# Retention in split halves from chunk 6 on instead of chunk 8, in a retention and two-layer feed-forward kernel

## The chip, the cores and the metric

The kernel runs on one core of one Trainium2 chip. The metric is the device time of one execution in microseconds (us); the figure to compare is the median of several executions. Profiles name the engines PE (TensorE matmul), PEld (TensorE weight load), DVE (VectorE), ACT (ScalarE), POOL (GpSimd) and SP (SyncE, which issues most DMAs).

## What is computed

Three stages, in fp32, follow one another:

```
state = gamma * state + k[t] (outer) v[t]          # retention, 4 batches, 8 heads, 768 steps, head size 64
y[t]  = scale * q[t] @ state
x = y as [3072, 512]
h = x @ w_in;  x = elu(h) @ w_out                  # first layer, 512 -> 2048 -> 512
h = x @ w2_in; x = (P(h) / Q(h)) @ w2_out          # second layer, P cubic, Q quadratic in |h|
```

Retention is worked in 24 chunks of 128 steps, six to a batch. Inside a chunk it is a masked product of queries and keys times the values, plus the queries times the state from the chunks before; the state is then decayed and the chunk's own key-value product added.

## The kernel before

The work is done in tiles of 512 tokens (`j`, 0 to 5; four chunks each) by 128 hidden units (`f`, 0 to 15). A step `it` of the first layer takes one pair (j, f) from a written list `seq`: (0, 0..5), then (1, 0..15), then (0, 6..15), then the other tiles. In a step TensorE does `g1` (12 products into `h`), then the second half of retention (`at_out`), then `g2` of the step before (12 products into four banks `acc`), then the first half of retention for the next half chunk (`at_in`). The order on every engine is the order in which the code issues; nothing is scheduled, and each engine takes its instructions in that order.

A half chunk, `i = 2 * chunk + g`, holds four heads. Halves 0 to 9 are done ahead of the first layer. Half 10 goes with step 0, 11 with step 1, 12 and 13 (chunk 6) with steps 2 and 3, 14 and 15 (chunk 7) with steps 4 and 5. Steps 6 to 21 carry no retention; from half 16 on it goes on later. Chunk 6 is the first of its batch, so it has no state to read; chunk 7 has one.

There are two forms. The early form (`c < LATE`, `c < EARLY`) multiplies in plain fp32, adds the decayed state on TensorE by a product with a diagonal matrix (L266), and ScalarE copies the sum back into `St` (L338). VectorE only masks the scores (L299). The late form splits each operand into a high and a low part in the fp32r type and takes three products of them (`gemm3`, L392). VectorE then multiplies the scores by the mask in place (L286), ScalarE rounds them to `Ah` (L289), VectorE subtracts to get `al` (L290) and makes the low parts of the queries of the next half (`qp`, L209, two instructions). It also updates `St` (L340 copies in a batch's first chunk, L342 after it) and joins the two parts of the output (L354, or L356 where there is no state). ScalarE and GpSimd split the keys (`kf`) and values (`vf`); SP loads `kr` and `kvs` for each half, one buffer each.

Beside this, weights arrive as float64 and VectorE narrows each 128x512 block in four instructions (L113, L114, L115, L117), ScalarE rounds it (L126) and GpSimd subtracts (L127). The list `nops` says how many of the four-instruction steps VectorE does in each step: 4, 5, 5, 6, 6, 6 in steps 0 to 5, and 5 in each of steps 6 to 17. Steps 6 to 11 use again the weights of f = 0 to 5. Each step's activation also needs VectorE once (L701, `t`), behind part of the narrowing, and ScalarE and GpSimd split its result to `gh` and `gl` for `g2`. Since the list leaves tile 0 after f = 5, its four banks `acc` are copied out in step 6, two by VectorE (L457); the next `g2` writes the same banks.

Of the kernel before, what the change touches and what calls it, by code (L numbers as in the profile page):

```python
# [9 lines left out]
F32 = mybir.dt.float32  # L10
F32R = mybir.dt.float32r
# [8 lines left out]
D = 64  # L20
C = 128
NP = H // 2
NW = 12
KD = 4
KF = 16
EARLY = 8
LATE = 8
LN2_63 = 63 * float(np.log(2.0))
TINY = 2.0 ** -63
QC = float(np.float32(1.0) + np.float32(1e-6))  # L30
# [19 lines left out]
def retention_ffn_kernel(ctx: ExitStack, tc: tile.TileContext, qkT, kv, w1i, w1o, w2i, w2o, a_, b_, tab, out):  # L50
    nc = tc.nc
# [16 lines left out]
    atw = at.enter_context(tc.tile_pool(name="atw", bufs=2))  # L68
# [84 lines left out]
    chk = {}  # L153

    def load_q(c):
        if c in (2, 3, 6, 7):
            qT = half[c % 4][:, 512:1024]
        else:
            qT = atw.tile([128, 512], F32, tag="qT", name="qT")
        chk[c] = (qT.rearrange("p (a t) -> p a t", a=NP),) + (kvb[c % 4] if c < LATE else (None,) * 3)  # L160
        nc.sync.dma_start(out=chk[c][0], in_=qkT[c, :, 0])

    def load_k(c):
        qT, vw, kw, kn = chk[c]
        if c >= LATE:
            return
        if c > 1:
            nc.sync.dma_start(out=kn, in_=kv[c, :, 0])
        for e in range(2):
            r = slice(64 * e, 64 * e + 64)  # L170
            (nc.scalar if 0 < c < 4 else nc.sync).dma_start(out=kw[r, e], in_=qkT[c, r, 1])
        if c < 2:
            nc.sync.dma_start(out=kn, in_=kv[c, :, 0])
        vf = vw.rearrange("p a f d -> p (a f d)")
        mid = kv[c, :, 1, 1:7, :].rearrange("p (a e) d -> p a (e d)", e=2)
        nc.sync.dma_start(out=vf[:, 128:704].rearrange("p (a n) -> p a n", a=3)[:, :, 0:128], in_=mid)
        nc.sync.dma_start(out=vf.rearrange("p (b d) -> p b d", d=D)[:, 0:12:11, :],
                          in_=kv[c, :, 1, 0:8:7, :])
# [5 lines left out]
    def scale_k(c):  # L184
        kn = chk[c][3]
        if c % CB != CB - 1 and c < LATE:
            nc.gpsimd.tensor_tensor(out=kn, in0=kn, in1=gk_t.to_broadcast([128, H, D]), op=ALU.mult)

    def load_kr(i):
        c, g = divmod(i, 2)  # L190
        if i < NI:
            nc.sync.dma_start(out=kr, in_=qkT[c, :, 1, 2 * g:2 * g + 2])

    def prep(i):

        c, g = divmod(i, 2)
        if c < LATE or i >= NI:
            return none
# [14 lines left out]
    def load_kv(i):  # L213
        c, g = divmod(i, 2)
        if LATE <= c < NCH:
            nc.sync.dma_start(out=knv, in_=kv[c, :, :, 4 * g:4 * g + 4])

    def scale_kn(i):
        c, g = divmod(i, 2)
        if LATE <= c < NCH and c % CB != CB - 1:  # L220
            nc.gpsimd.tensor_tensor(out=knv[:, 0], in0=knv[:, 0],
# [12 lines left out]
    def x_tile(j):  # L234
        if j not in x_t:
            n = XB[j] if j in XB else (j[1] + 1) % 2
            x_t[j] = tuple(xp.tile([128, KD, 512], F32R, tag=f"{nm}{n}", name=nm) for nm in ("xh", "xl"))
        return x_t[j]

    def at_in(i, early=False):  # L240
# [15 lines left out]
        def kv_sum():  # L256
            if c % CB != CB - 1:
                for p in (0, 1):
# [4 lines left out]
                    v2 = vw[:, 2 * g + p, 0:3:2, :]  # L263
                    old = c < EARLY and c % CB != 0
                    if old:
# [60 lines left out]
    def at_state(i):  # L326
# [3 lines left out]
        def part(e, p):  # L330
            r = slice(64 * e, 64 * e + 64)
            q = 2 * g + p
            d = slice(64 * e, 64 * e + 64)
            if c % CB == 0 or c < EARLY:
                if p == 0 and c % CB != CB - 1:
                    src, dst = so[r, 2:4, d], St[r, 2 * g:2 * g + 2, d]
                    if c < EARLY:
                        nc.scalar.copy(dst, src)  # L338
# [8 lines left out]
    def at_x(i):  # L347
        c, g = divmod(i, 2)
        sc, o = ps_t.pop(i)
        if c >= LATE:  # L350
            for e in range(2):
                r = slice(64 * e, 64 * e + 64)
                if c % CB:
                    nc.vector.tensor_tensor(out=o[r, 0:2, :], in0=su[r], in1=sc[r, e:4:2, :], op=ALU.add)  # L354
                else:
                    nc.vector.tensor_copy(o[r, 0:2, :], sc[r, e:4:2, :])  # L356
        xs = [x[:, 2 * g:2 * g + 2, c % 4 * C:c % 4 * C + C] for x in x_tile(c // 4)]
        nc.scalar.copy(xs[0], o[:, 0:2, :])
        nc.vector.tensor_tensor(out=xs[1], in0=o[:, 0:2, :], in1=xs[0].bitcast(F32), op=ALU.subtract)

    def run(steps):
        for x in steps:
            x()
# [30 lines left out]
    def g1(ps, f, xh, xl):  # L394
        wh, wl = W[f, "i"]
        pairs = []
        for kc in range(KD):
            s = slice(128 * kc, 128 * kc + 128)
            pairs += [(wh[:, s], xh[:, kc, :]), (wh[:, s], xl[:, kc, :]), (wl[:, s], xh[:, kc, :])]
        gemm3(ps, pairs, True, True)  # L400
# [99 lines left out]
    k0 = atw.tile([128, 1024], F32, tag="k0", name="k0", bufs=1)  # L500
    v0, v1 = (atw.tile([128, 768], F32, tag=nm, name=nm, bufs=1) for nm in ("v0", "v1"))
    n0 = atw.tile([128, 512], F32, tag="n0", name="n0", bufs=1)
# [54 lines left out]
    def abs_next():  # L557
        narrow_a(*todo[nabs[0]])
        nabs[0] += 1
# [19 lines left out]
    for i in range(10):  # L579
        c, g = divmod(i, 2)  # L580
# [25 lines left out]
        if i in (2, 3, 4, 5, 7, 8):  # L606
            ops, end = conv_next()
            ends.append(end)
    load_q(6)
    load_k(6)  # L610
    at_out(9)
    run(at_state(9))
    at_x(9)
    done()
    abs_next()
    nc.scalar.activation(out=b1, in_=ab[:, 5:6], func=ACTF.Abs)
# [3 lines left out]
    def load_c(f, e):  # L620
        c = tmp("wc")
        nc.sync.dma_start(out=c, in_=w2s[f][e])
        W[1, f, e, "c"] = c

    qp = atw.tile([128, 2, NP, C], F32R, tag="k0", name="qp", bufs=1)
    late_kv = atw.tile([128, 768], F32, tag="v0", name="kvs", bufs=1)
    knv = late_kv[:, 0:512].rearrange("p (b h d) -> p b h d", b=2, h=4)
    su = late_kv[:, 512:768].rearrange("p (a t) -> p a t", a=2)
    al = atw.tile([128, 4 * C], F32R, tag="n0", name="al", bufs=1)
    vf = None  # L630
    def first_late():

        load_q(LATE)
        load_kr(2 * LATE)
        load_kv(2 * LATE)
        for e in range(2):
            nc.gpsimd.memset(qp[64 - 64 * e:128 - 64 * e, e].bitcast(F32), 0.0)

    half0 = 6
    seq = [(0, f) for f in range(half0)] + [(1, f) for f in range(KF)] + [(0, f) for f in range(half0, KF)]  # L640
# [37 lines left out]
    for it, (j, f) in enumerate(seq):  # L678
        last = j == NB - 1
        xh, xl = x_t[j]  # L680
        both = j == 0 and (f < half0 or f >= KF - 8)
        at_a = both or (1 < j < NB - 1 and f % 2 == 0)
        at_b = both or (1 < j < NB - 1 and f % 2 == 1)
        h = psh.tile([128, 512], F32, tag="h", name="h")
        g1(h, f, xh, xl)
        n = nops[it]
        st = []
        if at_a:
            at_mask(nx[0])
            prep(nx[0] + 1)()  # L690
        narrow(min(n, 3))
        if at_a:
            st = attn_a()
        t = tmp("t", "t")
        nc.scalar.activation(out=t, in_=h, func=ACTF.Relu, scale=-1.0)  # L695
        nc.scalar.activation(out=t, in_=t, func=ACTF.Exp, scale=-1.0)  # L696
        finish()
        run(st)
        if at_a:
            at_x(nx[0])  # L700
        nc.vector.scalar_tensor_tensor(out=t, in0=t, scalar=-1.0, in1=h, op0=ALU.add, op1=ALU.max)  # L701
        gh = gp.tile([128, 512], F32R, tag="gh", name="gh")
        gl = gp.tile([128, 512], F32R, tag="gl", name="gl")
        nc.scalar.copy(gh, t)  # L704
        nc.gpsimd.tensor_tensor(out=gl, in0=t, in1=gh.bitcast(F32), op=ALU.subtract)  # L705
        if at_a:
            split_v(nx[0] + 1)
        narrow(max(n - 3, 0))
        abs_ahead((nops + [0])[it + 1])
        fill((3 if it < half0 + 8 else 1) - (1 if stream else 0))  # L710
        if last:
            split_w(1, f, 0)
            if f + 1 < KF:
                load_c(f + 1, 0)
            if f in (3, 6, 9, 12):
                load_x2(0, f // 3 - 1)
            if f in (4, 7, 10, 13):
                split_x2(0, f // 3 - 1)
        if pend is not None:
            g2(0, *pend)  # L720
        if at_b:
            attn_b()
        if last:
            if f:
                split_w(1, f - 1, 1)
            load_c(f, 1)
        if it < half0 + 8:
            fill(2 if stream else 3)
        elif not last and it not in tuple(range(19, 32)) + (47, 63, 79):
            fill(2)  # L730
        if it == 1:
            load_q(7)
            load_k(7)
        if it == 2:
            first_late()
        if it == 3:
            vf = atw.tile([128, 2, 4, D], F32R, tag="v1", name="vf", bufs=1)
        if (j, f) == (0, KF - 1):
            load_ya()
        if j == NB - 2 and f == KF - 1:  # L740
            load_c(0, 0)
        pend = (j, f, gh, gl)
# [40 lines left out]
    for j in range(NB):  # L783
        xh, xl = x_tile((1, j))
        for f in range(KF):
            h = ph.tile([128, 512], F32, tag="h2", name="h2")
            g1(h, f, xh, xl)
            a = rational_a1(h)
# [60 lines left out]
```

## Time and profile before

| | |
|---|---|
| median of 3 executions | 1185.8 us (1184.75 to 1186.55) |
| span of the profiled execution | 1184.0 us |
| TensorE busy | 1173.0 us, 99% of the span |
| VectorE busy | 896.9 us, 76% |
| ScalarE busy | 723.0 us, 61% |
| GpSimd busy | 487.5 us, 41% |

The span runs from the first to the last instruction of the profiled execution; the timed figures stand 1.8 us above it in the median. Shares of busy time are averages over the whole program; VectorE's is far higher in the first 165 us, where the weights of the first layer are narrowed.

### The profile page before, as it was taken

Reading aid. Unit: us, or ns where it says so; the run is one execution under the profiler, and the core shown is the slowest. Engines: PE = TensorE matmul, PEld = TensorE weight load, DVE = VectorE, ACT = ScalarE, POOL = GpSimd, SP = SyncE. Lnnn points to the kernel's source line nnn. Section 1 sums busy time; section 2 is a strip of 40 time slices with the busy share of each in tenths; the row PEclk is TensorE's granted clock in tenths of the full one; section 3 lists DMA queues with packets and bytes.
Section 4 is the critical chain, followed back from the end, with each engine's and each line's share of the span. In section 5 each row is a group of like instructions: output and inputs, shape, how many; then the busy total and the mean of one; then the engine's idle time right before and its main releaser. Section 6 shows DMA issues by size and latency. Waiting matters only on the chain.

```text
span 1184.0 us, 15783 instructions
## 1 busy us (share of the span) xinstructions
PE 1173.0 (99%) x5620; PEld 986.0 (83%) x5620; DVE 896.9 (76%) x1331; ACT 723.0 (61%) x1306; POOL 487.5 (41%) x415
## 2 busy tenths in 40 slices
PE   8999999999999999999999999999999999999998
PEld 7888888888888888888888888888888888888887
DVE  5979985776767677776565788888888888887876
ACT  2556655555555545554566776767777776767765
POOL 4556553554343444342588433232333232232222
PEclk8999999999999999999999999999999999999999
DMA  8654321233323232432455200200200200200101
GB/s 239 200 169 151 125 89 63 71 124 128 115 89 134 97 112 72 143 101 100 163 175 190 87 9 1 72 1 1 72 1 1 71 1 1 72 1 1 36 1 36
DMA packets 53135, 98.10 MB, mean 83 GB/s; under 512 B 7360, under 2 KB 23360, under 8 KB 53056
## 3 DMA queue, kind: packets, MB, share of 16 engines
q1 hardware_dynamic: 51856, 95.83, 24.8%
q10 hardware_dynamic: 1200, 1.26, 0.5%
q8 instruction: 44, 0.72, 0.2%
q14 instruction: 35, 0.29, 0.1%
HBM read 75.05 MB, written 22.02 MB: 82 GB/s over the span
## 4 chain that ended last, share of the span: by engine, by line
PE 94%; DVE 2%; DMA 1%; issue 1%; POOL 1%; ACT 1%; SPq 0%; DVEq 0%; ACTq 0%; POOLq 0%
PE acc L392 43%; PE h L392 43%; PE sc L392 4%; PE so L309 1%; PE so L260 1%; PE sc L278 1%; PE so L323 1%; DMA li<-in_qkT_dram 0%; DMA v<-in_kv_dram 0%; PE so L268 0%; POOL gl L705 0%; DMA k<-in_qkT_dram 0%; DVE qp L209 0%; DVE wc L117 0%; PE so L320 0%
## 5 line engine op out<-in xcount | busy, mean ns | idle before, releaser
L392 PE MATMUL h<-xh,wi 128*128 128x512 f32 x1536 | 507.2, 391 | 0.1
L392 PEld LDWEIGHTS h<-xh,wi 128*128 128x128 f32 x1536 | 288.3, 188 | 59.3 <-POOL wi L127 0.5
L392 PE MATMUL h<-xl,wi 128*128 128x512 f32 x768 | 299.2, 390 | 0.0
L778 POOL TENSOR_TENSOR gl<-e,gh 128x512 fp32r<-128x512 f32 x96 | 124.7, 1299 | 349.6 <-ACT gh L777 208.6
L705 POOL TENSOR_TENSOR gl<-t,gh 128x512 fp32r<-128x512 f32 x96 | 129.9, 1353 | 214.8 <-ACT gh L704 211.1
L392 PE MATMUL acc<-gh,wo 128*128 128x512 f32 x768 | 191.9, 392 | 0.1
L392 PE MATMUL acc<-wo,gh 128*128 128x512 f32 x768 | 190.2, 389 | 0.0
L392 PEld LDWEIGHTS acc<-wo,gh 128*128 128x128 f32 x768 | 144.1, 188 | 29.9
L392 PEld LDWEIGHTS h<-xl,wi 128*128 128x128 f32 x768 | 144.4, 188 | 29.1
L392 PEld LDWEIGHTS acc<-gh,wo 128*128 128x128 f32 x768 | 141.3, 188 | 29.2 <-ACT ys L466 0.9
L752 ACT ACTIVATE s<-h 128x512 f32<-128x512 f32 x96 | 57.4, 598 | 137.8 <-PE h L392 137.8
L704 ACT CAST gh<-t 128x512 fp32r<-128x512 f32 x96 | 59.7, 622 | 95.7 <-DVE t L701 95.7
L758 DVE SCALAR_TENSOR_TENSOR u<-s,b,u 128x512 f32<-128x512 f32 x96 | 71.9, 749 | 56.2 <-ACT u L753 55.6
L695 ACT ACTIVATE t<-h 128x512 f32<-128x512 f32 x96 | 57.6, 600 | 75.5 <-PE h L392 69.0
L392 PE MATMUL acc<-wo,gl 128*128 128x512 f32 x384 | 103.1, 389 | 0.0
L392 PE MATMUL acc<-gl,wo 128*128 128x512 f32 x384 | 103.0, 390 | 0.0
L701 DVE SCALAR_TENSOR_TENSOR t<-t,h 128x512 f32<-128x512 f32 x96 | 65.3, 680 | 45.5 <-ACT t L696 45.4
L768 DVE SCALAR_TENSOR_TENSOR e<-e,ab,r 128x512 f32<-128x512 f32 x96 | 72.3, 753 | 32.2 <-ACT r L762 32.2
L769 DVE SCALAR_TENSOR_TENSOR u<-u,r 128x512 f32<-128x512 f32 x96 | 87.6, 913 | 0.0
L113 DVE TENSOR_SCALAR wc<-wc 128x512 f32<-128x512 f32 x64 | 53.2, 831 | 43.4 <-ACT wc L100 43.3
L392 PEld LDWEIGHTS acc<-gl,wo 128*128 128x128 f32 x384 | 72.0, 188 | 15.6 <-POOL gl L705 0.2
L392 PEld LDWEIGHTS acc<-wo,gl 128*128 128x128 f32 x384 | 72.1, 188 | 15.0
(126 smaller groups left out, 1775.5 us busy)
## 6 DMA issues: line engine op xcount, KB each, us to landing
kvs<-in_kv_dram SPq DMA_DIRECT2D x33, 256.0 KB, 2.9
st<-in_w1i_dram SPq DMA_DIRECT2D x16, 512.0 KB, 3.5
st<-in_w1o_dram SPq DMA_DIRECT2D x16, 512.0 KB, 3.5
st<-in_w2i_dram SPq DMA_DIRECT2D x16, 512.0 KB, 4.6
st<-in_w2o_dram SPq DMA_DIRECT2D x16, 512.0 KB, 3.8
w2s<-wc SPq DMA_DIRECT2D x32, 256.0 KB, 3.5
wc<-w2s SPq DMA_DIRECT2D x32, 256.0 KB, 2.9
xs<-y SPq DMA_DIRECT2D x24, 256.0 KB, 3.9
```

What stands on the lines that cost most here:

```text
L113: lambda: v.tensor_scalar(c, c, F64_HI, F64_LO, op0=ALU.min, op1=ALU.max),
L260: nc.tensor.matmul(out=so[:, 2 + p, :], lhsT=knv[:, 0, 2 * p:2 * p + 2], rhs=knv[:, 1, 2 * p:2 * p + 2], start=True, stop=True)
L392: nc.tensor.matmul(out=ps, lhsT=lh, rhs=rh, start=first and idx == 0, stop=last and idx == len(pairs) - 1)
L695: nc.scalar.activation(out=t, in_=h, func=ACTF.Relu, scale=-1.0)
L701: nc.vector.scalar_tensor_tensor(out=t, in0=t, scalar=-1.0, in1=h, op0=ALU.add, op1=ALU.max)
L704: nc.scalar.copy(gh, t)
L705: nc.gpsimd.tensor_tensor(out=gl, in0=t, in1=gh.bitcast(F32), op=ALU.subtract)
L752: nc.scalar.activation(out=s, in_=ps, func=ACTF.Square)
L758: nc.vector.scalar_tensor_tensor(out=u, in0=s, scalar=b1, in1=u, op0=ALU.mult, op1=ALU.add)
L768: nc.vector.scalar_tensor_tensor(out=e, in0=e, scalar=ab[:, 0:1], in1=r, op0=ALU.add, op1=ALU.mult)
L769: nc.vector.scalar_tensor_tensor(out=u, in0=u, scalar=QC, in1=r, op0=ALU.add, op1=ALU.mult)
L778: nc.gpsimd.tensor_tensor(out=gl, in0=e, in1=gh.bitcast(F32), op=ALU.subtract)
```

## The change

Chunks 6 and 7, halves 12 to 15, take the late form instead of the early one. The tiles that the late form needs (`qp`, `kvs`, `al`, `vf`) take over buffers of chunks 4 and 5 earlier, the first loads of `q` and `kr` for chunk 6 stand ahead of step 0, and the loads and buffers of the early form for chunks 6 and 7 go.

```
-EARLY = 8
-LATE = 8
+EARLY = 6
+LATE = 6
...
-        if c in (2, 3, 6, 7):
+        if c in (2, 3):
             qT = half[c % 4][:, 512:1024]
...
-    load_q(6)
-    load_k(6)
     at_out(9)
     run(at_state(9))
     at_x(9)
...
     qp = atw.tile([128, 2, NP, C], F32R, tag="k0", name="qp", bufs=1)
...
     vf = None
-    def first_late():
-
-        load_q(LATE)
-        load_kr(2 * LATE)
-        load_kv(2 * LATE)
-        for e in range(2):
-            nc.gpsimd.memset(qp[64 - 64 * e:128 - 64 * e, e].bitcast(F32), 0.0)
+    load_q(LATE)
+    load_kr(2 * LATE)
+    for e in range(2):
+        nc.gpsimd.memset(qp[64 - 64 * e:128 - 64 * e, e].bitcast(F32), 0.0)
+    done()
...
+        if it == 1:
+            vf = atw.tile([128, 2, 4, D], F32R, tag="v1", name="vf", bufs=1)
...
-        if it == 1:
-            load_q(7)
-            load_k(7)
-        if it == 2:
-            first_late()
-        if it == 3:
-            vf = atw.tile([128, 2, 4, D], F32R, tag="v1", name="vf", bufs=1)
```

VectorE's order in step 4 (half 14, chunk 7), from the mask of one half to the mask of the next. Before (`A` is the masked score tile, `wc` a weight block, `xl` the low part of the output, `t` the activation):

```order
L299 TENSOR_TENSOR A<-sc,mask 128x512
L113 TENSOR_SCALAR wc<-wc 128x512
L114 TENSOR_SCALAR wc<-wc 128x512
L115 SCALAR_TENSOR_TENSOR wc<-st,wc 128x512
L359 TENSOR_TENSOR xl<-so,xh 128x2x128
L701 SCALAR_TENSOR_TENSOR t<-t,h 128x512
L117 SCALAR_TENSOR_TENSOR wc<-st,wc 128x512
L113 TENSOR_SCALAR wc<-wc 128x512
L114 TENSOR_SCALAR wc<-wc 128x512
L299 TENSOR_TENSOR A<-sc,mask 128x512
```

The same step in the changed kernel, where the activation's line number is 695:

```order
L286 TENSOR_TENSOR sc<-sc,mask 128x512
L290 TENSOR_TENSOR al<-sc,Ah 128x512
L209 TENSOR_TENSOR qp<-qT,qp 64x256 x2
L113 TENSOR_SCALAR wc<-wc 128x512
L114 TENSOR_SCALAR wc<-wc 128x512
L115 SCALAR_TENSOR_TENSOR wc<-st,wc 128x512
L342 SCALAR_TENSOR_TENSOR St<-St,tab_t,so 64x64 x4
L354 TENSOR_TENSOR so<-kvs,sc 64x256 x2
L359 TENSOR_TENSOR xl<-so,xh 128x2x128
L695 SCALAR_TENSOR_TENSOR t<-t,h 128x512
L117 SCALAR_TENSOR_TENSOR wc<-st,wc 128x512
L113 TENSOR_SCALAR wc<-wc 128x512
```

Nine instructions are new in the step (one `al`, two `qp`, four `St`, two `so`); all stand ahead of the activation `t`, and the narrowing keeps its places.

TensorE's order at the end of step 2 (`at_in` of half 13), between the last `g2` product and the next `g1`. Before (`li`, `lo` are weight buffers that hold the keys, queries and values of chunk 6):

```order
L392 MATMUL acc_647<-gl,wo_454 128x512
L392 MATMUL acc_648<-gl,wo_454 128x512
L278 MATMUL sc<-li_145,li_156 128x128 x4
L268 MATMUL so<-lo_154,li_145 128x128 x2
L392 MATMUL h<-xh,wi_629 128x512
```

And in the changed kernel:

```order
L392 MATMUL acc_659<-gl,wo_454 128x512
L392 MATMUL acc_660<-gl,wo_454 128x512
L392 MATMUL sc<-qp,kf 128x256 x6
L260 MATMUL so<-kvs 128x128 x2
L392 MATMUL h<-xh,wi_638 128x512
```

Six products of split parts stand in the place of four plain fp32 ones; the order around them is the same.

## Rows read from the trace of the kernel before

**Rows 1.** The profile page, the chain that ended last, by engine.

```profile
PE 94%; DVE 2%; DMA 1%; issue 1%; POOL 1%; ACT 1%; SPq 0%; DVEq 0%; ACTq 0%; POOLq 0%
```

**Rows 2.** Timeline of TensorE, steps 2 to 5: start, us, engine, line.

```profile
66.68 1.05 PE L278 MATMUL sc<-li,li 128*128 128x128 f32 x8
...
67.93 0.48 PE L392 MATMUL h<-xh,wi 128*128 128x512 f32 x1
...
74.38 1.05 PE L278 MATMUL sc<-lo,lo 128*128 128x128 f32 x8
...
76.08 0.48 PE L392 MATMUL h<-xh,wi 128*128 128x512 f32 x1
...
78.90 0.38 PE L320 MATMUL so<-lo,St 128*128 128x128 f32 x2
...
80.16 2.10 PE L392 MATMUL acc<-gh,wo 128*128 128x512 f32 x8
...
91.65 0.88 PE L392 MATMUL sc<-qp,kf 128*128 128x256 f32 x6
...
92.72 0.48 PE L392 MATMUL h<-xh,wi 128*128 128x512 f32 x1
```

**Rows 3.** Timeline of TensorE in a later step of tile 0.

```profile
209.93 0.60 PE L309 MATMUL so<-qT,St 128*128 128x128 f32 x4
...
211.08 2.01 PE L392 MATMUL acc<-gh,wo 128*128 128x512 f32 x8
```

**Rows 4.** Busy time of VectorE by stretch: length, busy, granted clock, DMA share.

```profile
60.00:92.70 32.70, 23.52 (x37) 1.00 0.53 169
...
101.00:141.00 40.00, 39.06 (x47) 1.00 0.42 144
```

**Rows 5.** Waits between 60 and 102 us: total, times, longest.

```profile
DVE xl L359 <- ACT xh L358: 8.1, 4, 3.5
...
DVE wc L113 <- ACT wc L100: 0.7, 1, 0.7
...
PEld acc L392 <- DVE li L457: 0.4, 1, 0.4
```

**Rows 6.** Timeline of VectorE in a later step of tile 0.

```profile
206.93 0.70 DVE L286 TENSOR_TENSOR sc<-sc,mask 128x512 f32<-128x512 f32 x1 [0.16 <-PE sc L392]
208.28 0.69 DVE L290 TENSOR_TENSOR al<-sc,Ah 128x512 fp32r<-128x512 f32 x1 [0.65 <-ACT Ah L289]
208.89 1.76 DVE L209 TENSOR_TENSOR qp<-qT,qp 64x256 fp32r<-64x256 f32 x2
210.98 1.17 DVE L342 SCALAR_TENSOR_TENSOR St<-St,tab_t,so 64x64 f32<-64x64 f32 x4 [0.33 <-ACT kvs L312]
212.25 0.90 DVE L354 TENSOR_TENSOR so<-kvs,sc 64x256 f32<-64x256 f32 x2
213.58 0.42 DVE L359 TENSOR_TENSOR xl<-so,xh 128x256 fp32r<-128x256 f32 x1 [0.44 <-ACT xh L358]
```

**Rows 7.** Timeline of VectorE in a half of a batch's first chunk.

```profile
257.21 0.59 DVE L340 COPY St<-so 64x128 f32<-64x128 f32 x2
```

**Rows 8.** VectorE by line and shape, 60 to 102 us: busy, mean ns, idle before.

```profile
L117 DVE SCALAR_TENSOR_TENSOR wc<-st,wc 128x512 int32<-128x512 int32 x7 | 8.2, 1166 | 0.2
...
L209 DVE TENSOR_TENSOR qp<-qT,qp 64x256 fp32r<-64x256 f32 x2 | 0.8, 414 | 0.0
```

**Rows 9.** The same view, 190 to 240 us.

```profile
L209 DVE TENSOR_TENSOR qp<-qT,qp 64x256 fp32r<-64x256 f32 x12 | 11.1, 927 | 0.1
```

**Rows 10.** Timeline of VectorE, one narrowing instruction at its shortest.

```profile
124.60 0.69 DVE L117 SCALAR_TENSOR_TENSOR wc<-st,wc 128x512 int32<-128x512 int32 x1
```

**Rows 11.** TensorE by stretch: length, busy, granted clock, DMA share, GB/s.

```profile
10.00:12.00 2.00, 0.69 (x3) 0.50 1.06 248
...
36.00:40.00 4.00, 3.20 (x28) 1.00 0.38 130
```

**Rows 12.** The profile page, DMA issues: count, KB each, us to landing.

```profile
kvs<-in_kv_dram SPq DMA_DIRECT2D x33, 256.0 KB, 2.9
```

More of the change, by code (lines that the diff above doesn't have):

```diff
@@ L613, in retention_ffn_kernel @@
     at_x(9)
+    qp = atw.tile([128, 2, NP, C], F32R, tag="k0", name="qp", bufs=1)
+    late_kv = atw.tile([128, 768], F32, tag="v0", name="kvs", bufs=1)
+    knv = late_kv[:, 0:512].rearrange("p (b h d) -> p b h d", b=2, h=4)
+    su = late_kv[:, 512:768].rearrange("p (a t) -> p a t", a=2)
+    al = atw.tile([128, 4 * C], F32R, tag="n0", name="al", bufs=1)
+    vf = None
+    load_q(LATE)
+    load_kr(2 * LATE)
+    for e in range(2):
+        nc.gpsimd.memset(qp[64 - 64 * e:128 - 64 * e, e].bitcast(F32), 0.0)
     done()
@@ L623, in load_c @@
         W[1, f, e, "c"] = c
[L625 to L630, printed above, removed]
-    def first_late():
-        load_q(LATE)
-        load_kr(2 * LATE)
-        load_kv(2 * LATE)
-        for e in range(2):
-            nc.gpsimd.memset(qp[64 - 64 * e:128 - 64 * e, e].bitcast(F32), 0.0)
     half0 = 6
```

## Prediction

> **What bounds the kernel now.** I read the page first: the chain that ended last runs through TensorE for 94% of the span [rows 1], so a saving on TensorE shows at once and work elsewhere shows only where TensorE comes to wait for it. The change lies in steps 2 to 5, between about 60 and 93 us, so I read that stretch as a timeline. TensorE goes through it without a gap: the reader can add its pieces from start to start in [rows 2]. Then I asked how much room the other engines have there. VectorE is busy 23.5 of the 32.7 us, and from 101 to 141 us, when only narrowing and activations are left, 39.1 of 40 [rows 4]. So VectorE's room before step 6 is nearly all there is. The waits say where it is: 8.1 us in four waits of `xl` for `xh` and 0.7 us in one of the narrowing for ScalarE [rows 5], 8.8 us in all. The last thing to see is how far TensorE may run ahead of VectorE. In step 6 the banks `acc` of tile 0 are copied out, and TensorE's weight load already waits 0.4 us for VectorE's copy L457 [rows 5]. VectorE has no slack at that point: a delay of L457 is a delay of TensorE.
>
> **What TensorE saves.** The first part of a half (`at_in`) takes 1.25 us in chunk 6 (66.68 to 67.93) and 1.70 us in chunk 7 (74.38 to 76.08), since there the two products with the diagonal come on top. In the late form it takes 1.07 us (91.65 to 92.72) [rows 2]. That is 2 x 0.18 + 2 x 0.63 = 1.6 us. The second part (`at_out`) with a state falls from 1.26 us (78.90 to 80.16) [rows 2] to 1.15 us (209.93 to 211.08) [rows 3]: 2 x 0.11 = 0.2 us. Chunk 6's second part I count as unchanged: four products and no state against six shorter ones. TensorE saves 1.8 us in all, and only if nothing makes it wait.
>
> **What VectorE gains.** All of it stands between the mask of half 12 and L457, in an engine that takes its instructions in order. For each of the four halves, from a step of the late form further on:
> - `al` and its wait: 0.65 us in which VectorE stands until ScalarE has rounded the scores, and 0.61 us from the start of `al` to the next instruction (208.28 to 208.89) [rows 6]; 4 x 1.26 = 5.0 us. The wait cannot go, since ScalarE's input is VectorE's mask, issued just ahead.
> - The low parts of the queries: the one pair that the kernel has in step 5 takes 2 x 0.414 us [rows 8], twelve further on 0.927 us each [rows 9]. In the late form the pair stands just where GpSimd splits keys, as in rows 9, so I take 2 x 0.927 for all four halves. Three pairs are new and one, in step 5, becomes longer: 3 x 1.85 + (1.85 - 0.83) = 6.6 us; with the short value 2.5 us. A fourth new pair, for half 12, falls into step 1, where the scaling of chunk 6's keys and its collisions go; I count these even.
> - The state: two copies, 0.6 us [rows 7], in each half of chunk 6, and 1.27 us (210.98 to 212.25) [rows 6] in each of chunk 7; 1.2 + 2.5 = 3.7 us. They were ScalarE's.
> - Joining the output: 0.90 us [rows 6]; four times 3.6 us. For chunk 6 it is two copies instead of two additions, counted alike.
>
> Together 5.0 + 6.6 + 3.7 + 3.6 = 18.9 us. Against it stands the room of 8.8 us, of which a wait of 0.44 us for `xh` [rows 6] is left in each half, 1.8 us: 7.0 us are taken up. L457 comes 18.9 - 7.0 = 11.9 us later, and TensorE with it. TensorE's own saving is not subtracted: it only reaches its wait earlier. Behind step 6 nothing gives the time back. VectorE is full to 141 us, and afterwards TensorE is the bound again, so the whole program stays 11.9 us late.
>
> The narrowing is the unknown. Its dearest instruction takes 0.69 us when nothing is in its way [rows 10] and 1.17 us in the mean here, seven times [rows 8]: 7 x 0.48 = 3.3 us of hindrance, when GpSimd works at the same time. In the late form GpSimd splits keys and values and scales queries, and no longer scales whole chunks of keys. I keep the means of before, and take 3.3 us less or more as the bounds.
>
> Edits counted at nothing. ScalarE gets the casts of scores, queries, keys and values and loses the state's copies; it waits for VectorE in these steps, and if it came late, the wait ahead of `al` or of the pair would show it, at 0.65 and 0.1 us in its rows [rows 6, 9]. The loads move as well: `kvs` and `kr` for each half stand on SP's queue, between the weight loads, and can only go when the half before is through with the buffer. They land 2.9 us after issue [rows 12] and have the rest of a step of some 8 us; without that cover, up to 2.9 us would be lost in each half, first in GpSimd's scaling of `kvs`, behind which the weights' and activation's low parts queue. The queries of chunk 6 now wait for chunk 4's buffer, and GpSimd's scaling of them stands ahead of step 0's `gl`; step 1's `g1`, of 2.8 us as in step 4 [rows 2], stands ahead of the `g2` that needs it and hides it; without that cover a landing of 2.9 us [rows 12] would be lost once.
>
> **Sum.** The profiled execution's span of 1184.0 us becomes 1195.9. The timed median, 1185.8, stands 1.8 us above that span; with the same distance I forecast 1197.7 us, 1.0% slower.
>
> **Rivals.**
> First, the products' saving shows and VectorE's work is absorbed: 1185.8 - 1.8 = 1184.0 us. Its place is L457. It holds if VectorE reaches it no later than now, that is, if the 18.9 us shrink to the 7.0 us of room. The short pair saves 4.1 us and narrowing without hindrance 3.3; 4.5 us would still be missing. For it speaks only that the room is uncertain; against it the 0.4 us that TensorE already waits [rows 5]. Even if true, it is 0.15% and hardly to be told from no change (measurements of this kernel tell differences from about 0.2%, 2.4 us).
> On the hindrance, the Trainium skill, page "SBUF — State Buffer", section "SBUF: two separate sides", says that VectorE and GpSimd hold a shared port pair in turn for a whole instruction. By it the hindrance can't vanish while GpSimd's splits are triggered in the same steps, and I gave this rival a lower chance than the rows alone would.
>
> Second, a mild form: the pair short and the narrowing less hindered, 11.9 - 4.1 - 3.3 = 4.5 us, 1190.3 us. For it, that the late rows come from steps with another mix on GpSimd; against it, that twelve of them have the long mean [rows 9].
>
> Third, TensorE's clock falls in a wait. At 10 to 12 us, where TensorE is busy 0.69 of 2 us after waiting for loads, the granted clock is 0.50, the lower of its two levels (1.2 of 2.4 GHz); at 36 to 40 us, with 3.20 of 4 us busy in short gaps, it stays 1.00 [rows 11]. The backlog makes TensorE wait about 11.9 / 4 = 3 us in a step, between the two. One `g1` at half the clock takes its 2.82 us (76.08 to 78.90) [rows 2] twice: one or two falls add 2.8 to 5.6 us, 1200.5 to 1203.3 us. The Trainium skill, page "TensorE: Matmul & The Clock Gate", section "What's actually happening", says that low activity takes the clock to half and activity gives it back; by it this case is open, the trace at 10 to 12 us agrees, and I give it one chance in ten.
>
> **How the numbers follow.** Forecast, 0.70: from 1193 to 1201.2 (11.9 plus 3.3 of hindrance above; the upper half of the pair's bounds below). Mild form, 0.07. Clock, 0.10. Absorbed, or so nearly that it stays within 2.4 us, 0.13, of which 0.03 would be faster by more than 0.2%, if the second parts of chunk 6 save too. So slower 0.87, same 0.10, faster 0.03. The range runs from the mild form, 1190, to the clock's 1203, which leaves out the absorbed case and a little above.
>
> **What would show it.** In the profile after: the waits of `xl` for `xh` fall from 8.1 us towards 1.8 us; VectorE has almost no other idle time between 60 and 105 us than the waits for `Ah`. TensorE gets gaps ahead of the products with `al` in steps 3 to 5 and ahead of `g2` in step 6, released by VectorE, of 10 to 14 us together with no such gap before; L457 moves from about 101 to about 113 us. The first parts of halves 12 to 15 take 1.07 us. The rest of the program has the same lengths, shifted. I am wrong if L457 stands near 101 us; if TensorE's gaps are released by GpSimd or by `kvs` (then loads and splits, not VectorE's added work, set the pace); or if the clock is below 1.00 behind 60 us.

## The result, and the profile after

The changed kernel takes 1201.12 us in the median of four executions (1198.66 to 1201.96), against 1186.07 us before: a ratio of 1.0118, with a 95% interval of 1.0106 to 1.0131. By the ratio the loss is 14 us; the two medians lie 15.1 us apart. The forecast was 1197.7 us in a range of 1190 to 1203. A second set of executions of the same kernel gave 1.0115 (1.0099 to 1.0132).

The page of the profile after, first the span and then the chain that ended last, by engine and by line:

```profile
span 1198.8 us, 15812 instructions
...
PE 90%; DVE 5%; issue 1%; ACT 1%; DMA 1%; POOL 1%; SPq 0%; DVEq 0%; ACTq 0%; POOLq 0%
PE acc L392 41%; PE h L392 41%; PE sc L392 4%; PE so L309 1%; PE so L260 1%; DVE wc L115 1%; DVE qp L209 1%; DVE wc L117 1%; PE so L323 1%; PE sc L278 0%; DMA k<-in_qkT_dram 0%; DMA v<-in_kv_dram 0%; POOL gl L699 0%; DVE St L342 0%; DVE wc L113 0%
```

VectorE's share of the chain goes from 2% [rows 1] to 5%, and the lines that carry it are the narrowing (L115, L117) and the low parts of the queries (L209), 1% each; the state (L342) is in it with less than half a per cent. The waits after, between 60 and 116 us, that is from half 12 to L457 (total, times, longest):

```profile
PE sc L392 <- DVE so L354: 6.2, 2, 3.4
DVE al L290 <- ACT Ah L289: 3.6, 4, 1.6
PE sc L392 <- DVE al L290: 3.4, 2, 1.9
PE sc L392 <- DVE so L356: 2.3, 1, 2.3
DVE xl L359 <- ACT xh L358: 1.8, 4, 0.4
DVE wc L113 <- ACT wc L100: 1.0, 1, 1.0
```

Before, TensorE waited for nothing here but 0.4 us for L457, and VectorE stood 8.8 us [rows 5]. Now TensorE waits 6.2 + 3.4 + 2.3 = 11.9 us for VectorE, and the wait for `xh` has fallen from 8.1 to 1.8 us. In the timeline of VectorE in step 4, from one mask to the next, and at L457, the reader sees an engine that stops only for two ScalarE casts, 0.65 and 0.44 us, and once for a weight:

```profile
84.12 0.70 DVE L286 TENSOR_TENSOR sc<-sc,mask 128x512 f32<-128x512 f32 x1
85.47 0.69 DVE L290 TENSOR_TENSOR al<-sc,Ah 128x512 fp32r<-128x512 f32 x1 [0.65 <-ACT Ah L289]
86.08 2.19 DVE L209 TENSOR_TENSOR qp<-qT,qp 64x256 fp32r<-64x256 f32 x2
...
91.08 1.15 DVE L342 SCALAR_TENSOR_TENSOR St<-St,tab_t,so 64x64 f32<-64x64 f32 x4
92.34 0.89 DVE L354 TENSOR_TENSOR so<-kvs,sc 64x256 f32<-64x256 f32 x2
93.67 0.42 DVE L359 TENSOR_TENSOR xl<-so,xh 128x256 fp32r<-128x256 f32 x1 [0.44 <-ACT xh L358]
94.02 0.68 DVE L695 SCALAR_TENSOR_TENSOR t<-t,h 128x512 f32<-128x512 f32 x1
...
96.32 0.69 DVE L113 TENSOR_SCALAR wc<-wc 128x512 f32<-128x512 f32 x1 [1.03 <-ACT wc L100]
...
97.92 0.70 DVE L286 TENSOR_TENSOR sc<-sc,mask 128x512 f32<-128x512 f32 x1
...
115.88 0.68 DVE L457 COPY li<-acc 128x512 f32<-128x512 f32 x1
```

Step 4 has 13.8 us from mask to mask (84.12 to 97.92). L457 stands at 115.88 us, where it stood at 100.81. Two us of that lie ahead of step 0, which begins at 49.08 us in this execution and at 47.04 before. Ahead of it the change moves only the first loads and clears for chunk 6. In the five profiles with the order of before (the kernel before and four runs below) step 0 begins between 46.31 and 49.00 us, 47.5 in the mean; in the seven with the changed order between 46.49 and 49.08, 47.7 in the mean. So I take the two us for chance and count from the beginning of step 0 to L457: 66.80 us here and 67.79 in the second profile, against 53.77, which is 13.0 and 14.0 us more. From there to the copy-out of the next tile (`ys`, near 186 us before) nothing changes: 151.82 from step 0, against 138.80, again 13.0 more.

### The profile page after: what moved, and what is told of

Read it like the earlier page. It is cut to its first block, busy times and chain, and to the rows that moved or that the text cites. A ratio compares the mean times of both kernels' runs of the same rounds, so it can differ in the third digit from the quotient of the medians.

```text
span 1198.8 us, 15812 instructions
## 1 busy us (share of the span) xinstructions
PE 1173.8 (98%) x5596; PEld 984.9 (82%) x5596; DVE 910.3 (76%) x1363; ACT 730.9 (61%) x1320; POOL 494.1 (41%) x425
## 3 DMA queue, kind: packets, MB, share of 16 engines
q10 hardware_dynamic: 1200, 1.26, 0.5%
## 4 chain that ended last, share of the span: by engine, by line
PE 90%; DVE 5%; issue 1%; ACT 1%; DMA 1%; POOL 1%; SPq 0%; DVEq 0%; ACTq 0%; POOLq 0%
PE acc L392 41%; PE h L392 41%; PE sc L392 4%; PE so L309 1%; PE so L260 1%; DVE wc L115 1%; DVE qp L209 1%; DVE wc L117 1%; PE so L323 1%; PE sc L278 0%; DMA k<-in_qkT_dram 0%; DMA v<-in_kv_dram 0%; POOL gl L699 0%; DVE St L342 0%; DVE wc L113 0%
## 5 line engine op out<-in xcount | busy, mean ns | idle before, releaser
L113 DVE TENSOR_SCALAR wc<-wc 128x512 f32<-128x512 f32 x64 | 50.0, 781 | 45.4 <-ACT wc L100 45.3
```

What stands on the lines that cost most here:

```text
L113: lambda: v.tensor_scalar(c, c, F64_HI, F64_LO, op0=ALU.min, op1=ALU.max),
```

## The experiments

Ten runs. For each profile the table gives the beginning of step 0, the start of L457, the distance between them, and the distance to the copy-out of tile 1, all us; and the timed ratio to the kernel before, run on the same chip. The bracket is what the distance to L457 has above that of the kernel before.

| kernel | step 0 | L457 | distance | to copy-out | timed ratio (95%) |
|---|---|---|---|---|---|
| before | 47.04 | 100.81 | 53.77 | 138.80 | 1 |
| changed | 49.08 | 115.88 | 66.80 (+13.0) | 151.82 | 1.0118 (1.0106 to 1.0131) |
| changed, again | 47.80 | 115.59 | 67.79 (+14.0) | 152.81 | 1.0115 (1.0099 to 1.0132) |
| state only, chunks 6 and 7 | 49.00 | 103.95 | 54.95 (+1.2) | 139.97 | 1.0009 (1.0000 to 1.0018) |
| state only, chunk 7 | 47.52 | 101.71 | 54.19 (+0.4) | 139.19 | 1.0002 (0.9993 to 1.0011) |
| products only | 48.15 | 113.81 | 65.66 (+11.9) | 150.67 | 1.0099 (1.0084 to 1.0114) |
| chunk 7 only | 47.61 | 110.79 | 63.18 (+9.4) | 148.19 | 1.0086 (1.0073 to 1.0100) |
| low parts on GpSimd | 46.88 | 112.44 | 65.56 (+11.8) | 150.60 | 1.0092 (1.0075 to 1.0109) |
| narrowing spread | 47.13 | 105.74 | 58.61 (+4.8) | 155.15 | 1.0120 (1.0105 to 1.0135) |
| before, half narrowing | 46.31 | 98.66 | 52.35 | 138.46 | 1.0002 (0.9993 to 1.0011) |
| changed, half narrowing | 48.31 | 104.85 | 56.54 | 142.64 | 1.0028 (1.0015 to 1.0041) |
| join first | 46.49 | 112.58 | 66.09 (+12.3) | 151.74 | 1.0103 (1.0080 to 1.0125) |

**Theory 1**, that of the prediction: VectorE's added work up to L457, less its room, is the loss. **Theory 2**, the rival that the waits after suggest: the products of a half and the scores of the next share one bank (`sc`), so a chain of scores, rounding, low part, second products and join sets the step, whatever else VectorE has to do.

### The change in its two halves

In the kernel before, the state alone:

```
-EARLY = 8
+EARLY = 6
```

> The kernel before with EARLY = 6 alone: chunks 6 and 7 keep the plain fp32 products, but VectorE keeps the state (two copies in each half of chunk 6, four updates in each of chunk 7) and TensorE's products with the diagonal go. Theory 1 (VectorE's added work in steps 2 to 5, less its room there, is what the time grows by): VectorE gains 0.7 + 0.7 + 1.26 + 1.26 = 3.9 us, less in each step than the wait of xl for xh there, so nothing is lost, and TensorE saves two diagonal products, 0.45 us, in each half of chunk 7: 0.9 us faster, 1185.2 us; L457 stays within 1 us of 100.8. Rival (the room is smaller than the waits say, any added VectorE work is paid in full): 3 to 4 us slower, about 1190.

Measured: 1187.62 us, ratio 1.0009; neither forecast. TensorE's saving does not show. The timeline of VectorE and then of TensorE:

```profile
66.14 0.59 DVE L340 COPY St<-so 64x128 f32<-64x128 f32 x2 [1.23 <-PE so L323]
67.84 0.42 DVE L359 TENSOR_TENSOR xl<-so,xh 128x256 fp32r<-128x256 f32 x1 [1.11 <-ACT xh L358]
...
95.41 0.68 PE L260 MATMUL so<-kvs 128*128 128x128 f32 x4 [1.31 <-DVE xl L359]
```

In step 2 the copy of the state stands 1.23 us behind TensorE's second products of the half. This costs nothing yet: `xl` comes 5.8 us after the mask of half 12, against 6.3 before. In step 5 VectorE is late enough that TensorE waits 1.31 us for `xl`. From start to start between the mask of half 12 and L457, the state adds 3.5 us, the narrowing takes 26.3 us instead of 24.4, and 4.2 of the idle 8.7 us are taken: 1.1 us, which is the distance's +1.2. So the expectation missed the narrowing, which it had left out.

> The kernel before with EARLY = 7 alone: only chunk 7's state goes to VectorE, chunk 6's copies stay on ScalarE. Theory 1: as with EARLY = 6, 0.9 us faster, 1185.2 us, since the copies of chunk 6 cost nothing in either place. Rival (added work is paid in full): 1.5 us slower.

With `EARLY = 7`, 1187.01 us, ratio 1.0002: no difference that can be told, and no gain either. TensorE waits 1.1 us for `xl` in step 5 here too.

The products alone, in the changed kernel:

```
-EARLY = 6
+EARLY = 8
...
                     if c >= LATE:
+                        old = c < EARLY and c % CB != 0
+                        if old:
+                            nc.tensor.matmul(out=so[:, 2 + p, :], lhsT=diag[:, 2 * g + p, :], rhs=St[:, 2 * g + p, :],
+                                             start=True, stop=False)
                         nc.tensor.matmul(out=so[:, 2 + p, :], lhsT=knv[:, 0, 2 * p:2 * p + 2],
-                                         rhs=knv[:, 1, 2 * p:2 * p + 2], start=True, stop=True)
+                                         rhs=knv[:, 1, 2 * p:2 * p + 2], start=not old, stop=True)
```

> The changed kernel with EARLY = 8 and the product with the diagonal added to the late form: chunks 6 and 7 use split products, but TensorE decays the state and ScalarE copies it, as before. Theory 1: VectorE loses 3.9 us of state work in steps 2 to 5, so L457 and the time come about 3.9 us sooner than in the changed kernel: 1197 us, still 1.0% above before. Theory 2 (the chain of the late form sets the step: scores, rounding, low part, second products, join, and only then the next scores, because one bank holds them all): the state is not in that chain, TensorE has 0.9 us more: 1201 to 1202 us.

Measured: 1198.88 us, ratio 1.0099, distance +11.9. So the split products bring nearly the whole loss, and the state 1 to 2 us of it; between the theories this run lies in the middle. The distance holds 0.9 us that step 0 and step 1 took longer than before (13.89 us to the mask of half 12, against 13.03; the granted clock was 0.67 from 45 to 50 us). From that mask to L457 the run is 2.1 us shorter than the changed kernel (51.77 against 53.87). That is less than the 3.9 us of VectorE's time that the state has, because the join now waits for ScalarE's copy of the state (waits between 40 and 120 us):

```profile
DVE so L360 <- ACT St L342: 1.9, 2, 1.1
```

The 3.9 us of work less 1.9 us of this wait are 2.0.

### One chunk instead of two

```
-EARLY = 6
-LATE = 6
+EARLY = 7
+LATE = 7
...
-        if c in (2, 3):
+        if c in (2, 3, 6):
...
+    load_q(6)
+    load_k(6)
...
+        if it == 1:
+            load_q(LATE)
+            load_kr(2 * LATE)
+            for e in range(2):
+                nc.gpsimd.memset(qp[64 - 64 * e:128 - 64 * e, e].bitcast(F32), 0.0)
```

> LATE = EARLY = 7: only chunk 7 (halves 14 and 15) takes the late form, and the first loads and clears for it stand at the end of step 1. Theory 1: per half 1.26 for al with its wait, 1.3 to 2.2 for a new pair, 1.26 for the state and 0.9 for the join, with one pair replaced: about 9.5 to 10.5 us, less the room that steps 3 to 5 have (1.3 + 1.8 + 0.7 + 1.4, less 0.9 that stays): 5 to 6 us slower than before, about 1191.5. Theory 2: half of the halves, half of the loss: 7 us, 1193.5.

Measured: 1196.92 us, ratio 1.0086, distance +9.4, well above both. Chunk 7 alone has 9.4 of the 13 us. Its waits between 60 and 111 us:

```profile
DVE xl L359 <- ACT xh L358: 5.5, 4, 3.5
PE sc L392 <- DVE so L354: 5.0, 2, 2.8
PE sc L392 <- DVE al L290: 1.9, 2, 1.4
DVE al L290 <- ACT Ah L289: 1.3, 2, 0.7
DVE wc L113 <- ACT wc L100: 1.0, 1, 1.0
DVE t L693 <- ACT t L688: 0.9, 1, 0.9
```

VectorE still stands 5.5 us for `xh`, 3.5 of them in one wait, in step 2. That room belongs to chunk 6's steps and can't be used in steps 4 and 5; there VectorE's waits for ScalarE even grow (1.0 and 0.9 us). The 0.9 us come from TensorE's clock: behind the wait of 2.8 us it was granted 0.50 from 101 to 103 us, the `g1` of step 6 took 3.8 us (101.72 to 105.53) instead of 2.8, and the activation behind it came late. I had subtracted 4.3 us of room; the run had 5.5 + 1.0 + 0.9 = 7.4 us of the 8.8 still idle, so only 1.4 us were taken. With it theory 1 gives 9.5 to 10.5 less 1.4, 8 to 9 us. The 3.6 us that chunk 6 adds are small because its halves take the large room of step 2 (one wait of 3.5 us here, 0.4 us in the changed kernel).

### VectorE's load changed, the chain kept

The low parts of the queries on GpSimd:

```
-                nc.vector.tensor_tensor(out=qp[r, e, 2:4, :], in0=qT[r, 2 * g:2 * g + 2, :],
+                eng = nc.gpsimd if i < 16 else nc.vector
+                eng.tensor_tensor(out=qp[r, e, 2:4, :], in0=qT[r, 2 * g:2 * g + 2, :],
```

> The changed kernel with the low parts of the queries (L209) of halves 12 to 15 on GpSimd instead of VectorE; nothing is left out. Theory 1 (VectorE's work sets the pace): VectorE loses three pairs of 1.3 to 2.2 us in steps 2 to 4 and one in step 1, and the pair of half 16 stays: about 5 us sooner at L457, 1196 us. Theory 2 (the late form's chain and its one bank of scores set the pace, with GpSimd's splits behind it): the pair is not in that chain, but GpSimd gets some 3 us per half more ahead of the weights' and the activation's low parts: no gain, 1201 us or slower.

Measured: 1197.57 us, ratio 1.0092, distance +11.8: 1 to 3 us of the 5 expected. Where the rest went shows in the narrowing's first instruction, 60 to 114 us (VectorE by line: busy, mean ns, idle). The changed kernel:

```profile
L209 DVE TENSOR_TENSOR qp<-qT,qp 64x256 fp32r<-64x256 f32 x8 | 5.8, 729 | 0.1
L113 DVE TENSOR_SCALAR wc<-wc 128x512 f32<-128x512 f32 x7 | 5.3, 751 | 1.1 <-ACT wc L100 1.0
```

And with the low parts on GpSimd, VectorE's line and then GpSimd's:

```profile
L113 DVE TENSOR_SCALAR wc<-wc 128x512 f32<-128x512 f32 x7 | 7.4, 1059 | 1.1 <-ACT wc L100 1.0
...
L210 POOL TENSOR_TENSOR qp<-qT,qp 64x256 fp32r<-64x256 f32 x6 | 6.2, 1041 | 0.2
```

GpSimd's 6.2 us hold up VectorE's narrowing: seven L113 take 2.1 us more, and all 28 narrowing instructions between the mask of half 12 and L457 take 26.8 us from start to start instead of 24.2. The wait for `Ah` grows by 1.1 us as well, so that 1.4 of the 4.9 us taken off VectorE are left. The Trainium skill's page "SBUF — State Buffer", section "SBUF: two separate sides", says that VectorE and GpSimd share a port pair, and that for instructions which need it the first to start holds it to its end while the other is blocked. The trace agrees: by the timelines nine of the changed kernel's 28 narrowing instructions meet no GpSimd instruction, and each takes its shortest time (0.42, 0.43 or 0.69 us); the other 19 take 8.8 us more together. With the low parts on GpSimd 23 of 28 meet one and take 11.3 us more.

The narrowing spread, eight instructions fewer in steps 0 to 5 and as many more in steps 6 to 20 (`nops` counts single instructions):

```
-    nops = [4, 5, 5, 6, 6, 6] + [5] * 12 + [4] * 3 + [0] * 11
+    nops = [4, 5, 4, 4, 4, 3] + [5, 5, 6] * 5 + [0] * 11
```

> The changed kernel with another list of narrowing steps: 24 instead of 32 in steps 0 to 5 (4, 5, 4, 4, 4, 3) and 5, 5, 6 in turn in steps 6 to 20, the same total. Theory 1: VectorE loses 8 narrowing instructions of about 0.8 us ahead of L457, which comes 6 us sooner; steps 6 to 20 get 8 more, but have only some 0.3 us of room each, so 2 to 4 us are given back by step 21, the rest stays: 1196 to 1199 us, with L457 near 110. Theory 2: the chain of the late form sets the length of steps 2 to 5 with or without narrowing: L457 stays near 116 us and the time at 1201 or above.

Measured: 1200.84 us, ratio 1.0120, no gain; but L457 comes 8 us sooner, at a distance of 58.61 instead of 66.80 us. The time is the one of theory 2, the place of L457 that of theory 1. The place tells the theories apart: if the chain alone had set steps 2 to 5, L457 would not have moved. The 8 us are lost again behind it. To the copy-out of tile 1 the distance is 155.15 us, 3.3 more than in the changed kernel. Between 106 and 200 us VectorE waits (first two rows) and TensorE waits (the others):

```profile
DVE wc L113 <- ACT wc L100: 5.1, 6, 1.3
DVE t L695 <- ACT t L690: 3.8, 2, 3.0
...
PE acc L392 <- ACT gh L698: 2.0, 4, 0.9
PE h L392 <- POOL wi L127: 1.1, 2, 0.6
PE h L392 <- ACT wi L126: 1.1, 1, 1.1
```

TensorE now meets late activations and late weights in steps 6 to 21. What I expected to be given back was 2 to 4 us; it was 11.5. The new list also costs VectorE 5.1 us of waits for ScalarE, which I had not counted. Some 1.6 us of the 11.5 are this execution's clock: it was 0.50 from 191 to 193 us, and the `g1` there took 3.7 us from its second piece to its last (190.38 to 194.12), against 2.2 in the changed kernel (190.59 to 192.76).

### Less narrowing, in both kernels

```
-        return [
+        ops = [
...
+        return [none, none] + ops[2:] if ph == 0 and f > 2 else ops
```

> The kernel before with the first two of the four narrowing instructions (L113, L114) left out for the first layer's weights from f = 3 on, so that its weights are not the right ones; the control for the next run. TensorE is the bound before, so both theories expect no change but for the 0.4 and 0.5 us that it waits for L457 and for the last weights: 1185 to 1187 us.

Measured: 1186.59 us, ratio 1.0002: as expected, TensorE is the bound before.

> The changed kernel with the same two narrowing instructions left out for the same weights (again not the right weights). Theory 1 (VectorE's total work up to step 21 is what delays TensorE): 16 instructions of 0.7 to 0.75 us, some 11 us, go in steps 0 to 5, and the steps behind get room as well: within 2 us of its control, 1184 to 1188 us. Theory 2 (the chain of the late form with its one bank of scores sets steps 2 to 5): most of the loss stays, 1195 us or more.

Measured: 1190.15 us, 3.6 us above its control, 4.2 by the distances to L457 and to the copy-out alike. Of a loss of 13 to 14 us, about 10 go with half of the narrowing; 3.6 to 4.2 stay, more than theory 1 forecast and far less than theory 2. The waits between 60 and 106 us say why some stays:

```profile
DVE al L291 <- ACT Ah L290: 4.4, 4, 1.3
PE sc L393 <- DVE so L355: 2.4, 2, 1.3
PE sc L393 <- DVE so L357: 2.1, 2, 1.3
```

TensorE still waits 4.5 us for the join. A step of the late form has no room for narrowing at all: without any, VectorE's chain from mask to mask fills all but 0.5 us of the 7.8 us that TensorE needs (206.93 to the next mask at 214.76 us before, in the stretch of [rows 6]; the 0.5 are its waits of 0.33 and 0.16 us there).

### The join moved forward

```
-        narrow(min(n, 3))
+        now = 0 if 2 <= it <= 5 else min(n, 3)
+        narrow(now)
...
-        narrow(max(n - 3, 0))
+        narrow(n - now)
```

> The changed kernel with all narrowing of steps 2 to 5 issued behind the join and the activation instead of up to three of it ahead of the state; the same instructions. TensorE waited 8.5 of its 12 us for the join (L354, L356), which now comes two to three instructions, about 2 us, earlier in each step. Theory 1: VectorE has the same total and no idle time to give, so L457 stays within 2 us of the changed kernel's and the time at 1199 to 1202 us; TensorE waits for the next scores' rounding and al instead. Theory 2 (the bank): up to 8 us faster, 1193 to 1196 us.

Measured: 1198.18 us, ratio 1.0103; the interval overlaps that of the changed kernel, so the gain of some 2 us is not certain. L457's distance is 66.09 us. The waits, 60 to 113 us:

```profile
PE sc L392 <- DVE al L290: 8.8, 3, 3.7
DVE al L290 <- ACT Ah L289: 4.1, 4, 2.2
DVE xl L359 <- ACT xh L358: 1.8, 4, 0.4
PE sc L392 <- DVE so L354: 0.7, 1, 0.7
```

The wait for the join is gone, 8.5 us to 0.7, and the wait for `al` takes its place, 3.4 to 8.8 us. Together they fall from 11.9 to 9.5 us; most of the rest went to waits for GpSimd and ScalarE (1.5 us). The shared bank decides mainly where TensorE waits, much less how long.

### The changed kernel again

> The changed kernel once more, for the spread between runs: the profiled run of it began step 0 2.0 us later than the kernel before (49.1 against 47.0 us), in code that the change does not touch. If that is chance, step 0 begins between 46.9 and 49.1 us, as in the other runs, and the distance from there to L457 is again about 66.8 us, 13 us above before. If the change causes it, step 0 begins near 49 us again.

Step 0 begins at 47.80 us and L457 is 67.79 us behind it: the 2 us ahead of step 0 were chance. The state-only run, which has the order of before there, began it at 49.00 us.

## Why the prediction was right, and where it was not

**The bound and the place.** Right: TensorE has no gap before, VectorE's room is in steps 2 to 5, and L457 has no slack. L457 is 13 to 14 us later from step 0, and so is all that follows, to within 0.1 us at the copy-out of tile 1.

**The sum.** 11.9 us forecast, 13.1 measured between the mask of half 12 (62.01 us after, 60.07 before) and L457, and 12.4 in the second profile. By its terms, from start to start:

| term, us | forecast | first profile | second profile |
|---|---|---|---|
| `al` with its wait | 5.0 | 6.1 | 5.2 |
| low parts of the queries | 6.6 | 5.2 | 6.1 |
| state | 3.7 | 3.9 | 3.9 |
| join | 3.6 | 3.6 | 3.6 |
| room taken | -7.0 | -5.9 | -5.2 |
| narrowing | 0 | -0.2 | -1.6 |
| masks (0.70 instead of 0.60 us each) | 0 | 0.4 | 0.4 |
| together | 11.9 | 13.1 | 12.4 |

`al` was taken too low for the first profile and the room too large for both, the low parts too high; these errors cancel in good part, so the nearness of the sum is partly luck. The room came out smaller because the wait for a weight stays (1.0 us) and, in the second profile, one for a late activation comes on top (0.7 us). The narrowing, the prediction's unknown, kept its time in the first profile (24.2 us against 24.4 before). The mechanism is that of theory 1, shown by L457 moving with the narrowing (58.61 against 66.80) and by the loss falling to 4 us with half of it.

The time itself, 1201.12 us, lies 3.4 us above the forecast and at the very edge of the range that was given 0.70, up to 1201.2; by its own sum, 1197.7 + 3.3, that edge is 1201.0. The first parts of halves 12 to 15, for which 1.07 us were expected, took 1.20, 2.01 (at the lower clock, below), 1.10 and 1.26 us, which changes nothing while TensorE waits anyway.

**The room.** Right in total, wrong as a single store. The chunk 7 run shows that it is each step's own: 5.5 us stayed idle there while L457 came 9.4 us later. The state-only run shows that work smaller than the room of every step can still cost time, 1.1 us, when the narrowing beside it gets longer.

**Where TensorE waits.** Wrong. I expected gaps ahead of the products with `al` and ahead of step 6's `g2`. Of 11.9 us, 8.5 stand ahead of the next half's first products, for the join, because one bank holds both; and no such gap stands ahead of `g2`, where the weight load waits 0.4 us for L457 as before. So L457 is a good mark for the delay and not the place where it arises. The size hangs little on it, as the join-first run shows.

**Nothing gives the time back.** Right, and stronger than I put it: even 8 us won by L457 are lost by step 21, because narrowing and activations fill VectorE to 185 us (busy 33.9 of the 35 us from 150 to 185). Up to there VectorE's total counts.

**The rivals.** That the work is absorbed did not happen. The mild form did not either. The clock did fall, between steps 2 and 3; a clock below 1.00 behind 60 us was one of the prediction's signs of being wrong. By stretch (length, busy time and count of TensorE, its weight loads, VectorE, ScalarE and GpSimd, then the granted clock):

```profile
70.00:80.00 10.00, 8.87 (x40) 7.72 (x41) 8.34 (x17) 5.48 (x13) 6.15 (x7) 0.83 0.43 127
```

Within it the clock was at 0.50, its lower level, from 72 to 74 us. I had priced one such fall at 2.8 us on top of the loss. In this execution it costs nothing that can be seen: the next thing that VectorE needs from TensorE are the scores for the mask at 73.27 us, and VectorE comes to it without idle time.

```profile
72.81 0.43 DVE L114 TENSOR_SCALAR wc<-wc 128x512 int32<-128x512 int32 x1
73.27 0.70 DVE L286 TENSOR_TENSOR sc<-sc,mask 128x512 f32<-128x512 f32 x1
```

Up to 81.25 us it stops only for its two casts, so a slower TensorE only used up its own wait. It is not free everywhere. In the second profile of the same kernel the clock fell at 71 us and once more, to 0.50 from 105 to 107 us; the scores and `g1` there end late, and VectorE waits for the activation just ahead of L457:

```profile
111.84 0.69 DVE L695 SCALAR_TENSOR_TENSOR t<-t,h 128x512 f32<-128x512 f32 x1 [0.69 <-ACT t L690]
```

With the 0.9 us in the chunk 7 run and some 1.6 in the spread run, a fall costs what VectorE, or TensorE behind it, then waits: 0 to 1.6 us in these rows, less than the 2.8 forecast. So part of the loss, up to 0.7 us in the second profile, is the third rival's.

**What stays open.** The two profiled executions are 14.8 and 14.6 us longer than the one before (1198.8 and 1198.6 against 1184.0): 2.0 and 0.8 us ahead of step 0, 13.0 and 14.0 from there to L457, and next to nothing behind. The extra us of the second arises in steps 0 and 1, which take 14.70 us to the mask of half 12, against 13.03 before and 12.93 in the first; VectorE goes through them without a wait. The prediction had counted the new pair of low parts in step 1 as even with what goes there. It was even in the first execution and cost time in the second, where the pair takes 1.77 us instead of 1.33 and two narrowing instructions behind it 2.5 us instead of 1.5. Why the executions differ in this, and why the clock falls in some waits and not in others, no run shows. No version here beats the kernel before.

## What to carry to other kernels

Before moving work to an engine, take its room step by step and not as a sum: idle time of one step is not there in the next when the engine takes instructions in order. Then take a mark at which the bound engine already waits for that engine, here L457. If that wait is not zero before, the work that exceeds the room up to the mark is lost time, and a saving on the bound engine showed nothing here. Look also at how long the engine stays full behind the mark, since work that is only put off comes back there: 8 us won at L457 were worth nothing at the end.

## What I had not expected of the hardware

The granted clock was 0.83 in the mean of a stretch of 10 us in which TensorE was busy 8.87, behind a wait of 2.3 us, whereas it stays 1.00 at 90 to 100 us, where TensorE is busy 4.72 of 10 us in the same kernel:

```profile
90.00:100.00 10.00, 4.72 (x26) 3.99 (x26) 7.63 (x15) 3.75 (x9) 3.11 (x4) 1.00 0.23 79
```

So in these rows the busy share of a stretch does not tell whether the clock falls in it. The length of the wait ahead does not either: in this profile waits of 3.4 and 2.8 us passed without a fall, and in the second profile the clock fell behind waits of 2.2 and 2.8 us and not behind one of 2.5. The same kernel falls at other places in another execution, and what it costs depends on who is last there.
